# Reordering the first batch of a pooled-attention, gMLP and expert kernel, and the start of its second stage

## The chip, the cores and the metric

The kernel runs on one core of a Trainium2 chip. The metric is the device time of one execution in microseconds (us), as the median of several runs. The engines are PE (TensorE, matmul), DVE (VectorE), ACT (ScalarE), POOL (GpSimd) and SP (SyncE, which only issues DMAs here).

## The reference

Three blocks follow one another, in fp32, for 8 batches of 576 tokens:

```python
def _attn_ref(q, k, v):                       # 8 heads of 64
    k_p = k.reshape(B, H, S // 8, 8, D).mean(axis=3)      # 72 pooled keys
    v_p = v.reshape(B, H, S // 8, 8, D).mean(axis=3)
    scores = 1 / np.sqrt(D) * np.matmul(q, k_p.transpose(0, 1, 3, 2))
    ...                                       # softmax
    return np.matmul(attn, v_p)

def _moe_ref(x, w_in, g_ln, w_sg, b_sg, w_out):           # x: 576 x 512
    h = gelu(x @ w_in)                        # 1024 columns
    u, v = h[..., :512], h[..., 512:]
    v_n = (v - mu) / np.sqrt(var + 1e-06) * g_ln
    v_s = np.einsum('ts,bsd->btd', w_sg, v_n) + b_sg[None, :, None]
    return x + (u * v_s) @ w_out

def _moe2_ref(x, w_gate, wq, wk, wv, wo):     # 4 experts, each a causal attention head
    logits = x @ w_gate                       # the two best experts of each token
    ...                                       # softmax over the two
    for e in range(E):
        q, k, v = x @ wq[e], x @ wk[e], x @ wv[e]
        ye = causal_softmax(q @ k.T / 8) @ v @ wo[e]
        out += weight_of_e * ye
```

## The kernel before

Every fp32 operand is split into a high and a low half, and a product is three matmuls (high by high, high by low, low by high). Names that end in h or l (x2h and x2l, wih and wil, vnh and vnl) are such halves.

The program has two stages. `PhaseA` does attention and the gMLP block batch by batch and writes its result, x2h and x2l, to DRAM. `PhaseB` reads that back and does the experts. Within a batch of `PhaseA` the work on PE is: scores of the next batch's attention, v's half of the input product, u's half (`upart`, `up` tiles, columns 0 to 3 called U0 to U3), the normalisation of v (`norm`), the spatial products d0 to d3 (`spatial`, `sp` tiles), and the four columns of the output product (`outp`, `op` tiles), between which the probabilities of the next batch are transposed (`trans`, `tr` tiles, tiles 0 to 4). Then the next batch's attention output (`av`) is multiplied, and the loop goes on.

Batch 0 has nothing before it, so its order is written by hand in the string `SEQ`. In it W0 to W7 split the input weights (`load64`: some DVE and ACT operations, the last of which, line 130, writes the low half; W3 is the last of them in the string, and U3 needs it), S0 to S4 load and split the spatial weights (`load_ws`; low halves by `tensor_sub` at line 163, on POOL or DVE by the string `SE`), k pools the keys of batch 1 on POOL (`pool_k`, lines 176 to 180, 4 instructions for each of two halves), o0 to o3 load pieces of the output weights and O0 to O3 split them, N0, N2, N4 are the normalisation of token tiles 0 and 1, 2 and 3, and 4, C0 to C4 are the scores of batch 1, X and F its softmax, P0 to P3 the spatial products, and R and v load and pool batch 1's values (two halves vraw, then vlraw).

A scheduler decides the order on each engine from the order of the code and from waits for buffers. Two pools matter here. The tag "raw" has three buffers, which the raw keys, the raw values and the pieces of the output weights take in turn, so that a load waits until an older tenant was used: the first v load of batch 1 takes over from piece O1 of the output weights, each v load after it waits for the pooling of one before, and the loads of batch 2's keys and values wait for the pooling of batch 1's. The tag "x2" has four, for x2h and x2l of two columns: column 2 can be written only when column 0 has left for DRAM. All these DMAs are issued by SP, in its queue's order.

The normalisation of a tile pair goes from DVE (statistics mv) to POOL (lines 391 and 392, the inverse deviation rs) to ACT (line 400, vnh) to DVE (line 402, vnl; for tile 4 line 404), and spatial product d0 needs them tile by tile.

`PhaseB` begins with the items of the string `PRE` (v0 to v4 are value projections, g the gate, 00 to 03 and 10 to 13 the projections of q in two halves and k in two halves for head pairs 0 and 1), then goes through units of scores (line 839), softmax, scaling (line 860), transposes (line 886) and products, with items of `FIRSTF` for batch 0 between them (x0 to x3 load the next batch's x).

Of the kernel before, what the change touches and what calls it, by code (L numbers as in the profile page):

```python
# [12 lines left out]
AF = mybir.ActivationFunctionType  # L13
# [16 lines left out]
FD = {(0, 0), (0, 1), (1, 3), (1, 4)}  # L30
XA = (0, 1, 2, 3)
VE = ('PPP', 'PPP')
KE = ('DD', 'PP')
SE = 'PDPP'
SEQ = ("a0 a1 b0 d0 b3 b1 b2 d1 b4 d2 c g p0 h0 h1 p1 h2 h3 s0 e0 f0 s1 e1 f1 s2 s3 e2 f2 e3 f3 "
       "s4 e4 f4 y0 y1 y2 t0 t1 t2 t3 t4 z l W0 U0 W1 U1 W2 U2 K Q k o0 o1 W4 Y0 W5 Y1 W6 Y2 W7 Y3 S2 S1 S0 "
       "V4 W3 N0 U3 S4 N2 S5 N4 S3 C0 C1 o2 O0 P0 C2 X0 X1 F0 o3 O1 P1 C3 F1 X2 O2 R P2 F2 X3 O3 "
       "P3 C4 F3 X4 v")
# [3 lines left out]
class PhaseA:  # L42
# [69 lines left out]
    def load64(self, tv, hi, lo):  # L112
# [16 lines left out]
        nc.vector.scalar_tensor_tensor(lf, zh, 2.0 ** 32, zl, op0=OP.mult, op1=OP.add)  # L129
        nc.vector.scalar_tensor_tensor(lo, lf, 2.0 ** -52, gf, op0=OP.mult, op1=OP.mult)  # L130

# [149 lines left out]
    def av(self, b, steps):  # L281
# [8 lines left out]
        for x in steps:  # L290
# [15 lines left out]
            for p in range(NP):  # L306
                if p in done and "r" in done and (b, p) not in self.X32:
                    self.put_x(b, p, ps[p])

    def put_x(self, b, p, ps):  # L310
# [11 lines left out]
        nc.vector.tensor_sub(fh[:, S:], ps[:, 1, HS - 64:HS], fh[:, 512:S].bitcast(F32))  # L322
        if b == 0 and p in XA:
            nc.scalar.activation(x32, ps[:, :, :HS], AF.Copy)  # L324
        else:
            nc.gpsimd.tensor_add(x32, xh.bitcast(F32), xl.bitcast(F32))
# [80 lines left out]
    def upart(self, b, f):  # L407
# [3 lines left out]
        for h in range(2):  # L411
            s = slice(h * HS, h * HS + HS)
            o = ps[:, h, :HS]
            for kc in range(4):
                xh, xl = self.XH[b, kc][:, s], self.XL[b, kc][:, s]
                nc.tensor.matmul(o, self.wi[0][:, kc, c], xh, start=kc == 0, stop=False)  # L416
                nc.tensor.matmul(o, self.wi[0][:, kc, c], xl, start=False, stop=False)  # L417
                self.upmm = nc.tensor.matmul(o, self.wi[1][:, kc, c], xh, start=False, stop=kc == 3).ins  # L418
# [49 lines left out]
    def run(self):  # L468
        self.weight_tiles()
        for b in range(B):  # L470
# [4 lines left out]
            else:  # L475
                self.middle(b)
            if n + 1 < B:
                self.load_k(n + 1)
                self.load_v(n + 1, 0)
                self.load_q(n + 1)  # L480
            ahead = 1 if b else 0
            for f in range(4):
                if more:
                    if f == 0:
                        self.finish(n, 4)
                    self.trans(n, f + ahead)
                self.outp(b, f)
            if more:
                if not ahead:
                    self.trans(n, 4)  # L490
                self.av(n, (0, "r", 2, 1, 3))

    def first(self):

        done = {}
        def after(i):
            return self.tc.issue_after(done[i]) if i in done else nullcontext()
# [6 lines left out]
        def pool_k1():  # L504
            with after(4):
                self.pool_k(1)
        def load_v1():
# [108 lines left out]
FILL = (('', '12 10 11', '', '13 x0 x1 x2 x3', '', '', 'o3 o1 o0', '', ''), ('v0', 'v1 00 02', '01 o2', '03', '', '', '', 'v2 v3', 'v4 g'))  # L616
FIRSTF = (('10', '11', '12', '13 x0 x1 x2 x3', '', '', '', '', ''), ('v0 00', '', '01 02 v1', '03', '', '', '', 'v2 v3', 'v4 g'))
LASTF = (('', '10 12 11', '', '', '13', '', 'o1', '', 'o0'), ('', '', '', '', '', 'o2', '', '', 'o3'))
SDF = {(0, 0), (0, 1), (0, 5), (0, 8), (1, 0), (1, 2), (1, 7)}
SDL = {(0, 4), (0, 6), (1, 6), (1, 7)}  # L620
PRE = 'v0 00 01 02 03 v1 v2 v3 v4 g'
AVS = [(0, 256), (256, S)]
# [394 lines left out]
```

## Time and profile before

| | |
|---|---|
| median of 3 runs | 958.4 us (958.32 to 1010.67) |
| profiled execution, its own time | 959.46 us |
| its span | 957.7 us |
| PE, busy | 911.7 us, 95% of the span |
| DVE, busy | 694.4 us, 73% |
| ACT, busy | 517.8 us, 54% |
| POOL, busy | 444.9 us, 46% |

The profiled execution lies 1.06 us above the median, and 1.8 us of it are outside the span. A busy engine is one that executes; what the idle time of an engine is worth depends on whether anything that ends last waits for it. The granted clock is a share of TensorE's full 2.4 GHz; 0.5 is its lower level, 1.2 GHz.

### The profile page before, as it was taken

What the parts mean: (1) busy time and instruction counts of PE and PEld (TensorE: products, weight loads), DVE (VectorE), ACT (ScalarE), POOL (GpSimd) and SP (SyncE); (2) the same over time, 40 slices, a digit from 0 to 9 for tenths busy, and PEclk for the clock granted to TensorE, in tenths of its full rate; (3) what the DMA queues carried; (4) which work ended last, traced back from release to release, by engine and by line L of the source; (5) the groups of instructions that cost most, each with busy time, mean ns of one, the idle gap of its engine ahead of it and who ended that gap; (6) DMA issues with size and microseconds to landing.
All of it is one profiled execution on the core that took longest, in us unless ns stands there. A gap on an engine that the chain in (4) does not pass through costs nothing.

```text
span 957.7 us, 18439 instructions
## 1 busy us (share of the span) xinstructions
PE 911.7 (95%) x6488; PEld 864.2 (90%) x6488; DVE 694.4 (73%) x1876; ACT 517.8 (54%) x1285; POOL 444.9 (46%) x621
## 2 busy tenths in 40 slices
PE   4897789999999999999999999899999999999997
PEld 3677769989989999899899899899999999999987
DVE  6998838757667577587576614897879797878785
ACT  3765334344343443343443433777778776867776
POOL 6555747558469368375583560122222222323221
PEclk9798989999999999999999999999999999999999
DMA  9601522312402404223116014525353534435121
GB/s 326 241 13 44 178 98 74 132 61 72 155 28 73 170 12 143 100 72 133 62 51 196 22 40 135 144 48 165 88 163 91 160 101 128 137 91 165 49 62 75
DMA packets 51644, 102.86 MB, mean 107 GB/s; under 512 B 10592, under 2 KB 16736, under 8 KB 50656
## 3 DMA queue, kind: packets, MB, share of 16 engines
q1 hardware_dynamic: 51408, 101.68, 33.2%
q8 instruction: 52, 0.85, 0.4%
q14 instruction: 40, 0.33, 0.1%
q10 hardware_dynamic: 144, 0.00, 0.0%
HBM read 59.72 MB, written 28.31 MB: 92 GB/s over the span
## 4 chain that ended last, share of the span: by engine, by line
PE 76%; DVE 11%; ACT 4%; POOL 3%; DMA 3%; issue 2%; SPq 1%; ACTq 0%; POOLq 0%; DVEq 0%
PE av L906 4%; PE sc L224 3%; PE op L457 3%; PE sp L434 3%; PE sp L433 3%; PE sp L432 3%; PE up L416 3%; PE up L418 3%; PE up L417 3%; PE op L458 3%; PE op L459 3%; PE vp L355 3%; PE vp L356 3%; PE vp L357 3%; PE t L886 3%; PE pj L715 2%
## 5 line engine op out<-in xcount | busy, mean ns | idle before, releaser
L860 POOL TENSOR_SCALAR pr<-pr,sm,gw 128x128 f32<-128x128 f32 (+3 forms) x119 | 72.2, 608 | 210.4 <-DVE sm L856 135.7
L844 ACT ACTIVATE pr<-s,sm 128x256 f32<-128x256 f32 (+4 forms) x160 | 83.0, 520 | 41.3 <-DVE sm L841 19.5
L432 PE MATMUL sp<-wsh,vnh 128*128 128x288 f32 x256 | 78.7, 308 | 3.9 <-ACT vnh L400 3.9
L457 PE MATMUL op<-g,woh 128*128 128x288 f32 x256 | 77.4, 306 | 3.8 <-DVE x2l L464 3.1
L416 PE MATMUL up<-x,wih 128*128 128x288 f32 x256 | 76.9, 300 | 1.5 <-ACT xu L324 1.5
L433 PE MATMUL sp<-wsh,vnl 128*128 128x288 f32 x256 | 77.0, 301 | 0.7 <-DVE vnl L402 0.6
L458 PE MATMUL op<-g,woh 128*128 128x288 f32 x256 | 76.1, 298 | 1.4 <-DVE g L445 1.4
L434 PE MATMUL sp<-wsl,vnh 128*128 128x288 f32 x256 | 76.7, 300 | 0.0
L418 PE MATMUL up<-x,wil 128*128 128x288 f32 x256 | 75.9, 296 | 0.7 <-DVE wil L130 0.7
L713 PE MATMUL pj<-xbh,wqh 128*128 128x288 f32 x256 | 75.5, 295 | 0.0
L715 PE MATMUL pj<-xbh,wql 128*128 128x288 f32 x256 | 75.5, 295 | 0.0
L714 PE MATMUL pj<-xbl,wqh 128*128 128x288 f32 x256 | 75.4, 295 | 0.0
L417 PE MATMUL up<-x,wih 128*128 128x288 f32 x256 | 75.1, 293 | 0.0
L459 PE MATMUL op<-g,wol 128*128 128x288 f32 x256 | 74.7, 296 | 0.0
L841 DVE CUSTOM_DVE_ANT_0 s<-s,mk 128x512 f32<-128x512 f32 (+3 forms) x128 | 62.4, 488 | 3.3 <-PE t L886 3.0
L891 DVE TENSOR_TENSOR pbl<-t,pbh 128x512 fp32r<-128x512 f32 (+3 forms) x128 | 60.5, 484 | 2.5 <-ACT pbh L890 0.9
L224 PE MATMUL sc<-kbd,qt 128*128 128x144 f32 (+1 forms) x320 | 50.4, 304 | 11.7 <-DMA qt<-q_in 8.5
L886 PE MATMUL t<-ident,pr 128*128 128x128 f32 x320 | 56.3, 277 | 3.3 <-POOL pr L860 3.1
L906 PE MATMUL av<-pbh,vt 128*128 128x320 f32 (+4 forms) x224 | 55.9, 279 | 2.7 <-ACT pbh L890 2.7
L464 POOL TENSOR_TENSOR x2l<-x2l,x2h 128x576 fp32r<-128x576 f32 x8 | 11.4, 1430 | 99.3 <-ACT x2h L463 99.3
L224 PEld LDWEIGHTS sc<-kbd,qt 128*128 128x128 f32 (+1 forms) x320 | 44.5, 192 | 14.4 <-issue 10.8
L400 ACT ACTIVATE vnh<-vg,rs 128x512 fp32r<-128x512 f32 (+1 forms) x40 | 27.2, 718 | 53.1 <-POOL rs L392 40.5
(247 smaller groups left out, 3352.4 us busy)
## 6 DMA issues: line engine op xcount, KB each, us to landing
kraw<-k_in SPq DMA_DIRECT2D x16, 576.0 KB, 3.8
x<-x2h SPq DMA_DIRECT2D x32, 288.0 KB, 2.1
x<-x2l SPq DMA_DIRECT2D x32, 288.0 KB, 2.1
xbl<-x SPq DMA_DIRECT2D x32, 288.0 KB, 4.1
xbh<-x SPq DMA_DIRECT2D x32, 288.0 KB, 4.0
kd<-scr SPq DMA_DIRECT2D x64, 144.0 KB, 2.5
out<-o SPq DMA_DIRECT2D x32, 288.0 KB, 3.8
vraw<-v_in SPq DMA_DIRECT2D x16, 512.0 KB, 4.1
```

Source lines behind the costliest of these rows:

```text
L224: nc.tensor.matmul(ps[:m, p // 2, (p % 2) * 144:(p % 2) * 144 + 144], qt[:, p, o:o + m], kbd[:, p, :], start=p % 2 == 0, stop=True, skip_g ...
L416: nc.tensor.matmul(o, self.wi[0][:, kc, c], xh, start=kc == 0, stop=False)
L417: nc.tensor.matmul(o, self.wi[0][:, kc, c], xl, start=False, stop=False)
L418: self.upmm = nc.tensor.matmul(o, self.wi[1][:, kc, c], xh, start=False, stop=kc == 3).ins
L432: nc.tensor.matmul(o, vh[:, k, c], self.ws[0][:, k, s], start=k == 0, stop=False)
L433: nc.tensor.matmul(o, vl[:, k, c], self.ws[0][:, k, s], start=False, stop=False)
L434: nc.tensor.matmul(o, vh[:, k, c], self.ws[1][:, k, s], start=False, stop=False)
L457: nc.tensor.matmul(o, self.wo[0][:, k, c], gh[:, s], start=k == 0, stop=False)
L458: nc.tensor.matmul(o, self.wo[0][:, k, c], gl[:, s], start=False, stop=False)
L459: nc.tensor.matmul(o, self.wo[1][:, k, c], gh[:, s], start=False, stop=k == 3)
L715: nc.tensor.matmul(ps, self.wq[1][:, kc, c], xh[:, s], start=False, stop=kc == 3)
L906: nc.tensor.matmul(ps[:, s - lo:], vt[:, j, 2 * p + e].rearrange("p a d -> p (a d)"), t[:, e, j * PTS + s:j * PTS + up], start=j == 0 and ...
```

## The change

In batch 0, the pooling of batch 1's keys (k) goes behind W3 in `SEQ` and waits there for W3's last DVE operation, by way of two small copies on DVE into the raw keys; load o1 goes with it. The low halves of the spatial weights are all computed on DVE (`SE`). The copies of x that the residual uses (x32, line 324) are written after all of `av`. The loads of batch 2's keys, values and queries are written behind the columns of the output product, not ahead of them. For every batch `upart` takes its four row blocks in the order 2, 0, 1, 3. The second stage begins with all value projections and the gate, then the keys, then the queries and pair 1's queries, and its first units lose three fillers.

```diff
-SE = 'PDPP'
+SE = 'DDDD'
...
-       "s4 e4 f4 y0 y1 y2 t0 t1 t2 t3 t4 z l W0 U0 W1 U1 W2 U2 K Q k o0 o1 W4 Y0 W5 Y1 W6 Y2 W7 Y3 S2 S1 S0 "
-       "V4 W3 N0 U3 S4 N2 S5 N4 S3 C0 C1 o2 O0 P0 C2 X0 X1 F0 o3 O1 P1 C3 F1 X2 O2 R P2 F2 X3 O3 "
+       "s4 e4 f4 y0 y1 y2 t0 t1 t2 t3 t4 z l W0 U0 W1 U1 W2 U2 K Q o0 W4 Y0 W5 Y1 W6 Y2 W7 Y3 S2 S1 S0 "
+       "V4 W3 k o1 N0 U3 S4 N2 S5 N4 S3 C0 C1 o2 O0 P0 C2 X0 X1 F0 o3 O1 P1 C3 F1 X2 O2 R P2 F2 X3 O3 "
...
-        nc.vector.scalar_tensor_tensor(lo, lf, 2.0 ** -52, gf, op0=OP.mult, op1=OP.mult)
+        self.cv = nc.vector.scalar_tensor_tensor(lo, lf, 2.0 ** -52, gf, op0=OP.mult, op1=OP.mult).ins
...
+        for p in range(NP if b == 0 else 0):
+            self.nc.scalar.activation(self.X32[b, p], ps[p][:, :, :HS], AF.Copy)
...
-        if b == 0 and p in XA:
-            nc.scalar.activation(x32, ps[:, :, :HS], AF.Copy)
-        else:
+        if b:
             nc.gpsimd.tensor_add(x32, xh.bitcast(F32), xl.bitcast(F32))
...
-            for kc in range(4):
+            for kc in (2, 0, 1, 3):
...
-            if n + 1 < B:
-                self.load_k(n + 1)
-                self.load_v(n + 1, 0)
-                self.load_q(n + 1)
+            def loads():
+                if n + 1 < B:
+                    self.load_k(n + 1)
+                    self.load_v(n + 1, 0)
+                    self.load_q(n + 1)
+            if b:
+                loads()
...
                 self.outp(b, f)
+            if not b:
+                loads()
...
         def pool_k1():
-            with after(4):
-                self.pool_k(1)
+            with self.tc.issue_after(self.cv):
+                for t in self.RAW["k", 1].values():
+                    self.nc.vector.tensor_copy(t[:, 0, 0, :2], t[:, 0, 0, :2])
+            self.pool_k(1)
...
-FIRSTF = (('10', '11', '12', '13 x0 x1 x2 x3', '', '', '', '', ''), ('v0 00', '', '01 02 v1', '03', '', '', '', 'v2 v3', 'v4 g'))
+FIRSTF = (('', '12', '', '13 x0 x1 x2 x3', '', '', '', '', ''), ('v0 00', '', '01 02 v1', '03', '', '', '', 'v2 v3', 'v4 g'))
...
-PRE = 'v0 00 01 02 03 v1 v2 v3 v4 g'
+PRE = 'v0 v1 v2 v3 v4 g 02 03 00 01 10 11'
```

What this does to the order on the engines is seen at three places. On POOL, in batch 0, around the pooling of batch 1's keys (kraw into kbd), the low halves of the spatial weights (wsl) and the first normalisation (rs); the list of before begins with the second half of the keys, ahead of which the same rows stand once more for the first half:

```order
L176 TENSOR_TENSOR kraw<-kraw 128x576
L177 TENSOR_TENSOR kraw<-kraw 128x288
L180 TENSOR_TENSOR kbd_96<-kraw 64x2x72 x2
L163 TENSOR_TENSOR wsl<-st_594,wsh 128x576
L163 TENSOR_TENSOR wsl<-st_602,wsh 128x576
L163 TENSOR_TENSOR wsl<-st_704,wsh 128x576
L391 TENSOR_SCALAR rs<-mv 128x2
L392 TENSOR_TENSOR rs<-rs,mhalf 128x2
```

After:

```order
L175 TENSOR_TENSOR kraw<-kraw 128x576 x2
L176 TENSOR_TENSOR kraw<-kraw 128x288 x2
L179 TENSOR_TENSOR kbd_96<-kraw 64x2x72 x4
L390 TENSOR_SCALAR rs<-mv 128x2
L391 TENSOR_TENSOR rs<-rs,mhalf 128x2
```

The three weight operations have left POOL, and the pooled keys (both halves, eight instructions) stand directly ahead of the first rs, which was behind the weights.

On SP, in batch 0, after the last piece of the output weights, before (vraw and vlraw are batch 1's values in the first two rows; kraw, the vraw rows behind it and qt are batch 2's; x_0_57 is the DRAM buffer of batch 0's x2):

```order
L71 DMA vraw<-v_in 128x1024 x2
L75 DMA vlraw<-vl_in 128x512
L58 DMA kraw<-k_in 128x1152 x2
L71 DMA vraw<-v_in 128x1024
L65 DMA qt<-q_in 128x2304
L71 DMA vraw<-v_in 128x1024
L466 DMA x_0_57<-x2h 128x576
L466 DMA x_0_57<-x2l 128x576
```

After:

```order
L70 DMA vraw<-v_in 128x1024 x2
L74 DMA vlraw<-vl_in 128x512
L64 DMA qt<-q_in 128x2304
L57 DMA kraw<-k_in 128x1152 x2
L70 DMA vraw<-v_in 128x1024
L465 DMA x_0_57<-x2h 128x576
L465 DMA x_0_57<-x2l 128x576
L70 DMA vraw<-v_in 128x1024
```

The queries went ahead of batch 2's keys, and the first x2h and x2l ahead of the last value load; the other loads still stand ahead of the write-back.

On SP at the start of the second stage, before (kd is a copy of the projected keys of a head pair, four DMAs; qz pieces of the queries; xbh and xbl the loads of batch 1's x):

```order
L737 DMA qzvhi_6015<-qs_6007 64x512
L737 DMA qzvlo_6016<-qs_6007 64x512
L751 DMA kd<-scr 64x576 x4
L737 DMA qzvn_6017<-qs_6011 64x512
L737 DMA qzgln<-qs_6011 64x512
L642 DMA xbh<-x_1_58 128x576
L751 DMA kd<-scr 64x576 x4
L643 DMA xbl<-x_1_58 128x576 x2
L644 DMA xbh<-x_1_58 128x64
```

After:

```order
L757 DMA kd<-scr 64x576 x4
L743 DMA qzvhi_6017<-qs_6009 64x512
L743 DMA qzvlo_6018<-qs_6009 64x512
L743 DMA qzvn_6019<-qs_6013 64x512
L743 DMA qzgln<-qs_6013 64x512
L648 DMA xbh<-x_1_58 128x576
L650 DMA xbh<-x_1_58 128x64
L649 DMA xbl<-x_1_58 128x576 x2
L757 DMA kd<-scr 64x576 x4
```

The first kd moved ahead of the queries' pieces, and the second behind two more of the loads of x.

## Rows read from the trace of the kernel before

**Rows 1.** Busy time, granted clock and transfers in five stretches (engine: us, instructions).

```profile
76.00:83.20 7.20, 6.54 (x25) 5.96 (x26) 6.41 (x13) 5.59 (x20) 0.11 (x1) 0.54 0.01 1
83.20:120.20 37.00, 30.66 (x224) 28.95 (x223) 32.18 (x58) 15.53 (x50) 27.06 (x36) 1.00 0.45 149
120.20:123.90 3.70, 0.05 (x1) 0.00 (x0) 1.12 (x3) 0.65 (x1) 0.00 (x0) 1.00 0.74 288
123.90:131.00 7.10, 7.06 (x34) 5.42 (x35) 2.06 (x5) 1.66 (x3) 1.53 (x2) 0.53 0.39 149
...
300.00:500.00 200.00, 200.00 (x1414) 188.84 (x1414) 136.81 (x233) 79.94 (x115) 130.11 (x180) 1.00 0.26 89
```

**Rows 2.** What PE waited for from 30 to 150 us: us, times, longest.

```profile
PE sp L432 <- ACT vnh L400: 3.9, 2, 3.4
PE tr L275 <- DVE ptl L278: 3.7, 1, 3.7
PE op L457 <- DVE x2l L464: 2.8, 1, 2.8
PE up L416 <- ACT xu L324: 1.5, 1, 1.5
```

**Rows 3.** PE in order of time: start us, us, work, idle before it and releaser.

```profile
79.93 0.61 PE L435 MATMUL sp<-wsh,vnh 128*128 128x288 f32 x1 [0.41 <-DVE vnh L404]
...
132.58 0.40 PE L355 MATMUL vp<-wih,x 128*128 128x512 f32 x1
```

**Rows 4.** POOL in order of time, same columns.

```profile
30.42 1.88 POOL L176 TENSOR_TENSOR kraw<-kraw 128x576 f32<-128x576 f32 x1
...
37.76 1.09 POOL L180 TENSOR_TENSOR kbd<-kraw 64x144 f32<-64x144 f32 x2
52.37 11.77 POOL L163 TENSOR_TENSOR wsl<-st,wsh 128x576 fp32r<-128x576 f32 x3 [13.51 <-ACT xu L420]
67.07 0.63 POOL L391 TENSOR_SCALAR rs<-mv 128x2 f32<-128x2 f32 x1 [2.93 <-DVE mv L390]
...
102.15 1.27 POOL L191 TENSOR_TENSOR vraw<-vraw 128x512 f32<-128x512 f32 x1
...
106.49 0.99 POOL L198 TENSOR_TENSOR vlo<-vraw,vhi 64x128 fp32r<-64x128 f32 x2
...
111.28 1.40 POOL L176 TENSOR_TENSOR kraw<-kraw 128x576 f32<-128x576 f32 x1 [0.20 <-DMA kraw<-k_in]
...
113.63 1.04 POOL L180 TENSOR_TENSOR kbd<-kraw 64x144 f32<-64x144 f32 x2
```

**Rows 5.** DVE in order of time, same columns.

```profile
52.73 0.75 DVE L163 TENSOR_TENSOR wsl<-st,wsh 128x576 fp32r<-128x576 f32 x1
...
64.35 0.68 DVE L130 SCALAR_TENSOR_TENSOR wil<-st,g 128x512 fp32r<-128x512 f32 x1
...
79.12 0.75 DVE L404 SCALAR_TENSOR_TENSOR vnh<-vg,rs,vnh 64x512 fp32r<-64x512 f32 x1
...
85.26 0.69 DVE L130 SCALAR_TENSOR_TENSOR wol<-st,g 128x512 fp32r<-128x512 f32 x1
...
154.46 3.65 DVE L404 SCALAR_TENSOR_TENSOR vnh<-vg,rs,vnh 64x512 fp32r<-64x512 f32 x1 [1.53 <-ACT vnh L400]
```

**Rows 6.** ACT in order of time, same columns.

```profile
122.08 0.65 ACT L463 ACTIVATE x2h<-op 128x576 fp32r<-128x576 f32 x1 [4.26 <-DMA x<-x2h]
```

**Rows 7.** SP's DMA issues in order of time: start, us of the issue, transfer.

```profile
115.08 0.42 SPq L466 DMA_DIRECT2D x<-x2h  x1
```

**Rows 8.** The page's DMA issues over the whole span: median us from issue to landing.

```profile
kraw<-k_in SPq DMA_DIRECT2D x16, 576.0 KB, 3.8
x<-x2h SPq DMA_DIRECT2D x32, 288.0 KB, 2.1
...
vraw<-v_in SPq DMA_DIRECT2D x16, 512.0 KB, 4.1
```

**Rows 9.** What PE waited for from 575 to 700 us.

```profile
PE t L886 <- POOL pr L860: 2.4, 3, 1.0
```

More of the change, by code (lines that the diff above doesn't have):

```diff
@@ L30 @@
 FD = {(0, 0), (0, 1), (1, 3), (1, 4)}
-XA = (0, 1, 2, 3)
 VE = ('PPP', 'PPP')
 KE = ('DD', 'PP')
-SE = 'PDPP'
+SE = 'DDDD'
 SEQ = ("a0 a1 b0 d0 b3 b1 b2 d1 b4 d2 c g p0 h0 h1 p1 h2 h3 s0 e0 f0 s1 e1 f1 s2 s3 e2 f2 e3 f3 "
-       "s4 e4 f4 y0 y1 y2 t0 t1 t2 t3 t4 z l W0 U0 W1 U1 W2 U2 K Q k o0 o1 W4 Y0 W5 Y1 W6 Y2 W7 Y3 S2 S1 S0 "
-       "V4 W3 N0 U3 S4 N2 S5 N4 S3 C0 C1 o2 O0 P0 C2 X0 X1 F0 o3 O1 P1 C3 F1 X2 O2 R P2 F2 X3 O3 "
+       "s4 e4 f4 y0 y1 y2 t0 t1 t2 t3 t4 z l W0 U0 W1 U1 W2 U2 K Q o0 W4 Y0 W5 Y1 W6 Y2 W7 Y3 S2 S1 S0 "
+       "V4 W3 k o1 N0 U3 S4 N2 S5 N4 S3 C0 C1 o2 O0 P0 C2 X0 X1 F0 o3 O1 P1 C3 F1 X2 O2 R P2 F2 X3 O3 "
        "P3 C4 F3 X4 v")
@@ L413, in upart @@
             o = ps[:, h, :HS]
-            for kc in range(4):
+            for kc in (2, 0, 1, 3):
                 xh, xl = self.XH[b, kc][:, s], self.XL[b, kc][:, s]
-                nc.tensor.matmul(o, self.wi[0][:, kc, c], xh, start=kc == 0, stop=False)
+                nc.tensor.matmul(o, self.wi[0][:, kc, c], xh, start=kc == 2, stop=False)
                 nc.tensor.matmul(o, self.wi[0][:, kc, c], xl, start=False, stop=False)
```

## The prediction

> **What bounds the kernel now.** I read the table of stretches first, for what PE does. In the steady batches it has no gap: from 300 to 500 us it is busy for 200.00 of 200 us at a granted clock of 1.00 [rows 1]. Nothing that the change does to DVE, POOL or the transfers there can shorten the run unless it takes PE work away, and it takes none. So I went to the places where PE waits, which are batch 0 and the start of the second stage. PE's waits up to 150 us name four [rows 2]: 3.9 us in the normalisation (ACT's vnh), 3.7 us once for a low half of the transposed probabilities (ptl), 2.8 us for x2l in the output columns, 1.5 us for a copy of x ahead of U0. Then the clock: from 76 to 83.2 us it is 0.54 and from 123.9 to 131 us 0.53, each time just after a long wait of PE, while the stretch between, with the wait of 2.8 us in it, stays at 1.00 [rows 1]. A stretch of 7.06 busy us at 0.53 costs 7.06 x 0.47 = 3.3 us. The second long wait together with its clock is thus worth 3.7 + 3.3 = 7.0 us, the largest single thing that the change could take.
>
> What ends that second wait is a transfer. ACT had nothing to do for 4.26 us until x2h of column 0 had reached DRAM [rows 6], since column 2 takes its buffer; DVE's x2l and the ptl behind it in DVE's queue came after that, and PE's transposes after those. The DMA had been issued at 115.08 us [rows 7], so that it took almost 7 us, where the median over the run is 2.1 [rows 8]: the loads of batch 2 were ahead of it, 1.2 MB of queries among them. And it was issued that late because SP stood at a value load that waits for pooled keys, which POOL finished at 113.63 + 1.04 = 114.67 us [rows 4].
>
> **The copies of x and the order of the row blocks: 0.** On ACT the copies stand in the same sequence before and after, and U0 waits in both for the same one, since it frees U0's PSUM tile. The bound below is the whole 1.5 us; above it is small, because the block that is asked for first is ready first.
>
> **Spatial weights on DVE: 0 on the path.** DVE gets three more of 0.75 us [rows 5], 2.25 us; POOL loses one stretch of 11.77 us [rows 4]. The low half of W3 ended at 64.35 + 0.68 = 65.03 us [rows 5], after a stretch in which DVE shared time with those POOL operations. How much DVE gets back there has no row; the same line 404 takes 0.75 us alone and 3.65 us beside POOL's value pooling [rows 5], so between nothing and more than the 2.25 us. I take W3's end at 64 us (bounds 63 and 67.3). Either way U3 ends before PE must wait for the normalisation, so the gain is covered by that wait.
>
> **Pooled keys behind W3: +1.5 on the first spatial product.** They were done in the shadow of batch 0's attention, 30.42 to 38.85 us, 8.4 us for eight instructions; a single half alone in a later batch took 111.28 to 114.67, which makes 6.8 for two [rows 4]. Now they start on POOL at about 64.2 and end between 71.0 and 72.6. Behind them in POOL's queue is the first rs, which began at 67.07 [rows 4], and behind that the chain vnh, vnl, the aggregation for the next pair, rs, vnh, vnl, and the same for tile 4, whose low half was ready at 79.12 + 0.75 = 79.87 us and which PE took at 79.93 [rows 3, 5]. The scores of batch 1 wait for the keys as well. Not all of the 3.9 to 5.5 us arrives: about 2 us of statistics stood between and are now ahead of the first vnl on DVE. I count 9 us from the end of the first rs (72.4 to 74.3) to the last low half, 81.4 to 83.3 us, so +1.5 to +3.4, and I take the lower end because DVE is less disturbed than before (bounds 0 and +5.5). PE is idle meanwhile, which costs the clock as before; that is no new loss.
>
> **Output weights, value pooling and write-back: -2.8 for the first batch.** Since the pieces of w_out come later, their splitting moves behind d0 and d1 on DVE. The last operation of O1 was over at 85.95 us [rows 5]; in the new order it stands behind d1's product, two reductions of scores and its own four operations, which brings it to 94.8. The first value load waits for exactly that. From there: a v load of 4.1 us [rows 8] to 98.9; pooling, 102.15 to 107.48 before, so 5.3 us [rows 4], to 104.2; the second v load to 108.3; pooling to 113.6; batch 2's keys, 3.8 us [rows 8], to 117.4; their first half pooled, 3.4 us, at 120.8. Before it was 114.67, so this chain on POOL and SP slides by 6 us. Only the first pair of x2 profits from standing ahead of the last value load: it waits for vlraw's pooling instead, some 115.5 us, and is issued at about 116, hardly another moment than 115.08. But the queries have been loaded by then, so I give it 4 us in place of 7, and the transposes of tile 4 begin near 122 and not at 123.9, some half us after the columns (120.2 + 1.5). The second pair is issued at 121.3 and needs between 2.1 (the median) and 4.1 us (a v load is just ahead); with 3.1 it lands at 124.4. The last column's sum on DVE needs its buffer, and the ptl of tile 4 stands behind that sum: 1.5 us, 125.9. Now the rest of av. Before, from the end of the wait to the first matmul of batch 1's v at 132.58 [rows 3] there were 8.7 us, 5.4 without the clock's 3.3, 0.5 of them transposes; 32 of av's 40 matmuls now stand behind the last ptl, so 0.8 x 4.9 = 3.9 us, if the clock stays up. That gives 129.8 in place of 132.58: -2.8. I take the clock as staying up, since two short waits of 0.5 and some 2 us take the place of one of 3.7, and after the one of 2.8 us in the columns it was 1.00 [rows 1, 2]. The bounds are -7.0 (wait and clock wholly gone) and +3 (this chain later by another 3 us and the clock low as before).
>
> **Second stage: -1.2.** PE has the same matmuls. Its waits there for scaled scores of POOL sum to 2.4 us in three pieces, the longest 1.0 [rows 9]. With the gate's small operations out of DVE's way earlier, the first units should be scaled sooner; but the second pair's kd now stands behind more loads on SP. Bounds -2.4 (all of it) and +1.0 (one more wait like the longest); I take half the gain.
>
> **Sum.** 0 + 0 - 2.8 - 1.2 = -4.0 us (the +1.5 is inside the chain). The profiled execution took 959.46 us, which gives 955.5; the median lies 1.06 lower, so I forecast **954.4 us**, with 952 to 956.5 for this case, chance 0.40.
>
> **The rivals.** *The POOL chain keeps pace.* If O1 is split earlier than I count, the loads and both x2 pairs are on time, the whole 7.0 us goes: 958.4 - 7.0 - 1.2 = 950.2. For it speaks that DVE is less disturbed, against it that four splits now crowd behind d0. Chance 0.18. *The second stage gives nothing or loses up to 1.0*, because the kd copies come later: 955.6 to 956.6; chance 0.16. *The change does not do what it says*: the order shows that most loads are still ahead of the write-back, so the wait of 3.7 us and the low clock may simply stay; then only -1.2, 957.2. Chance 0.10.
>
> *Slower: the pooled keys are held up on POOL.* They now run beside DVE's statistics and normalisation, with the first rs right behind them. The row against them is the three weight operations, 3.92 us each [rows 4] beside a busy DVE, where the first step of pooled keys, of the same 128x576, took 1.40 [rows 4], 2.8 times less. Each us by which they end later moves d0, O1, the value loads and the end of av by one. From +2.8 the first batch gains nothing, and if PE's wait there is then as long as the two after which the clock was low, its 3.3 us are lost too: with +4, -2.8 + 4 + 3.3 - 1.2 = +3.3, 961.7 us; chance 0.12. With the whole factor of 2.8 they take 19 in place of 6.8 us, +12.2, which makes -2.8 + 12.2 + 3.3 - 1.2 = +11.5, 969.9; chance 0.04. Against it stands that in batch 0's attention the same keys needed only 8.4 us beside a DVE at work.
>
> [...]
>
> **How the numbers follow.** 949 to 960.5 us should hold the time 8 times in 10: it takes in the forecast, the first three rivals and the mild half of a late chain, and leaves out most of the slow rival and a second stage at its lower bound on top of the whole 7.0. Two per cent is 19 us here, about what a measurement of this kernel can tell from no change; no case reaches it but something unforeseen, so 0.02 for faster, 0.96 for within, 0.02 for slower.
>
> **What would show it right or wrong.** In the profile after: pooled keys on POOL near 64 to 72 us and the first rs directly behind; d0 about 1.5 us later; the first x2h issued near 116 and the second near 121; no wait of PE over 3 us between 118 and 126 and a clock near 1.00 behind it; batch 1's v at about 129.8; the second stage's waits for line 860's successor about halved. The prediction is wrong if the normalisation ends much beyond 83 us, if the second pair of x2 comes past 123, or if the clock is low behind the columns once more.

## The result: slower by about one per cent

The changed kernel took 971.85 us (median of 3 runs, 969.26 to 973.09) where the kernel before took 958.4. The ratio, on record as of fast runs without the slow one of 1010.67 us, is 1.0112 with an interval of [1.0087, 1.0137]; that of the two medians would be 1.014. The forecast was 954.4 us, in a range up to 960.5: the time lies outside it, on the other side of no change.

The profiled execution, the slowest of the three, took 973.09 us with a span of 971.3, 13.6 more than that of before. It splits in two at points that both traces have. Batch 1's first matmul of v begins at 141.04 us, 8.46 later than in [rows 3]. The second stage begins at 591.92 us and not at 583.40, which is the same 8.5, so nothing is lost or won in the batches between. The second stage itself then lasts 379.4 us in place of 374.3, 5.1 more, in this execution.

Line numbers after the change are mostly lower by one up to the loads, and higher by six in the second stage. First PE, of its waits from 40 to 160 us those that answer to [rows 2] or are new (us, times, longest), and its first matmul of batch 1's v:

```profile
PE sc L223 <- POOL kbd L179: 2.8, 1, 2.8
PE av L295 <- DVE x2l L461: 2.7, 1, 2.7
PE op L456 <- DVE x2l L463: 2.4, 1, 2.4
PE sp L434 <- DVE vnh L403: 2.4, 1, 2.4
...
PE tr L274 <- DVE ptl L277: 1.6, 1, 1.6
```

```profile
141.04 0.40 PE L354 MATMUL vp<-wih,x 128*128 128x512 f32 x1
```

The wait of 3.7 us for ptl is down to 1.6, as hoped. But 2.8 us for the pooled keys are new, and the wait of `av` for x2l (2.7) stands where that of ptl stood. No wait is over 3 us any more, and yet everything is late. So I looked where the time of the first spatial product went, on POOL (start us, us, work, idle before and releaser):

```profile
65.31 2.82 POOL L175 TENSOR_TENSOR kraw<-kraw 128x576 f32<-128x576 f32 x2 [33.41 <-DVE kraw L511]
...
70.49 2.14 POOL L179 TENSOR_TENSOR kbd<-kraw 64x144 f32<-64x144 f32 x4
72.72 0.23 POOL L390 TENSOR_SCALAR rs<-mv 128x2 f32<-128x2 f32 x1
...
127.15 1.03 POOL L179 TENSOR_TENSOR kbd<-kraw 64x144 f32<-64x144 f32 x2
```

The pooled keys take 65.31 to 72.63 us, eight instructions in 7.3 us, and the first rs, at 67.07 in [rows 4], follows at 72.72. On DVE the last low half of the normalisation ends at 83.28 + 0.74 = 84.02 us (79.87 in [rows 5]), and piece O1 of the output weights ends at 98.91 (85.95):

```profile
83.28 0.74 DVE L403 SCALAR_TENSOR_TENSOR vnh<-vg,rs,vnh 64x512 fp32r<-64x512 f32 x1
...
98.24 0.67 DVE L129 SCALAR_TENSOR_TENSOR wol<-st,g 128x512 fp32r<-128x512 f32 x1
...
133.70 0.76 DVE L461 TENSOR_TENSOR x2l<-op,xu 128x576 f32<-128x576 f32 x1 [3.72 <-DMA x<-x2h]
```

The last of these rows shows what is left of the write-back: the last column's sum waits 3.72 us for a transfer of x2. Its DMA was issued at 128.59 us, the first of the pair's two, so about 5 us before. On DVE the pair's low half, and on SP the DMAs:

```profile
120.81 0.76 DVE L463 TENSOR_TENSOR x2l<-op,x2h 128x576 fp32r<-128x576 f32 x1 [0.78 <-ACT x2h L462]
```

```profile
121.22 0.42 SPq L465 DMA_DIRECT2D x<-x2h  x1
...
128.21 0.33 SPq L70 DMA_DIRECT2D vraw<-v_in  x1
128.59 0.43 SPq L465 DMA_DIRECT2D x<-x2h  x1
```

In [rows 7] the first x2h was issued at 115.08; now it is 121.22. The second pair was ready at 120.81 + 0.76 = 121.57, and stood for 7 us in SP's queue behind the value load that waits for the pooled keys (127.15 + 1.03 = 128.18). Last, the stretches that answer to [rows 1] (busy us and instructions of PE, PEld, DVE, ACT and POOL, granted clock, DMA share, GB/s):

```profile
71.50:84.00 12.50, 8.17 (x32) 6.38 (x32) 8.20 (x16) 5.08 (x8) 4.59 (x9) 0.73 0.25 84
...
119.30:126.40 7.10, 7.10 (x44) 7.08 (x45) 3.48 (x7) 2.06 (x3) 3.64 (x8) 0.76 0.80 248
126.40:130.10 3.70, 2.12 (x17) 1.89 (x16) 1.42 (x3) 0.65 (x1) 1.65 (x3) 1.00 0.64 185
130.10:134.50 4.40, 1.73 (x10) 1.18 (x10) 0.80 (x2) 0.45 (x2) 0.00 (x0) 0.86 0.93 342
134.50:141.00 6.50, 6.49 (x35) 5.66 (x36) 2.26 (x6) 2.53 (x4) 3.13 (x3) 0.57 0.26 101
```

From 76 to 83.2 us the clock was 0.54 before [rows 1], and from 71.5 to 84 it is 0.73 now. Later it is low twice: 0.76 with PE busy for all of 119.3 to 126.4 us, and 0.57 while the last matmuls of `av` run. The low clock that the change was to save is still there, and a second, milder one has come ahead of it.

### The profile page after: what moved, and what is told of

Same layout as the page of the kernel before. It is cut to its first block, busy times and chain, and to the rows that moved or that the text cites. A ratio compares the mean times of both kernels' runs of the same rounds, so it can differ in the third digit from the quotient of the medians.

```text
span 971.3 us, 18445 instructions
## 1 busy us (share of the span) xinstructions
PE 916.7 (94%) x6488; PEld 869.7 (90%) x6488; DVE 691.0 (71%) x1881; ACT 518.1 (53%) x1285; POOL 431.8 (44%) x618
## 4 chain that ended last, share of the span: by engine, by line
PE 75%; DVE 10%; ACT 4%; DMA 4%; issue 3%; POOL 2%; SPq 1%; ACTq 0%; DVEq 0%; POOLq 0%
PE sc L223 4%; PE av L912 4%; PE op L456 3%; PE sp L432 3%; PE sp L433 3%; PE sp L431 3%; PE up L415 3%; PE up L417 3%; PE up L416 3%; PE op L457 3%; PE op L458 3%; PE vp L354 3%; PE vp L355 3%; PE vp L356 3%; PE t L892 2%
## 5 line engine op out<-in xcount | busy, mean ns | idle before, releaser
L275 ACT ACTIVATE pth<-tr 128x640 fp32r<-128x640 f32 (+1 forms) x40 | 26.2, 654 | 57.6 <-PE tr L274 48.0
```

## The experiments

The theory after this result was that the pooled keys cost the time, since they were taken out of the shadow of batch 0's attention and now stand ahead of the first rs. The rivals were the weights (with what they do to the order on SP), the strings of the second stage, and the copies and loads. Each expectation names its theories in its own words. The kernel before, run beside these, had medians of 959.95 to 960.84 us, and all but one of its single runs lay between 955 and 965; so a time read from one profile is worth less than a ratio over several runs.

**The weights alone** (`weights_alone`):

```diff
-SE = 'PDPP'
+SE = 'DDDD'
```

> The kernel before with only the string SE changed: all low halves of the spatial weights on DVE; the pooled keys stay where they were. Theory A (the first batch loses its 8.5 us because the pooled keys stand ahead of the first rs): the value loads and the write-back change places as in the changed kernel, but the normalisation ends at about 80 us as before, and the time is within 2 us of before, 956 to 960. Theory B (the loss comes from the pieces of the output weights being split later on DVE, so that the first value load of batch 1 and all that POOL does after it slide): most of the 8.5 us is here already, 964 to 967, with O1's last operation at 95 us or later.

It took 962.15 us, ratio 1.0031 [1.0011, 1.0051]. The order shows that this one string also makes the later changes on SP: queries ahead of keys, and the first x2 pair ahead of the last value load. DVE and SP in order of time:

```profile
81.03 0.76 DVE L438 TENSOR_TENSOR xu<-sp,xu 128x576 f32<-128x576 f32 x1 [0.96 <-PE sp L436]
...
92.08 0.68 DVE L130 SCALAR_TENSOR_TENSOR wol<-st,g 128x512 fp32r<-128x512 f32 x1
```

```profile
121.11 0.43 SPq L466 DMA_DIRECT2D x<-x2h  x1
```

d0's product with u (line 438, the first work behind d0) starts at 81.03 us; before it was 83.87:

```profile
83.87 0.76 DVE L438 TENSOR_TENSOR xu<-sp,xu 128x576 f32<-128x576 f32 x1 [1.40 <-PE sp L436]
```

So the weights help the normalisation, by 2.8 us in this pair of profiles. Over all profiles the gain is smaller and less sure: d0's product starts at 80.84 and 84.06 in the two other kernels below with only the weights' side of the front changed, and at 82.92 to 85.01 in four with the front as before. But O1 ends 6.8 us later than in [rows 5] all the same, because its operations now stand behind d0 and, most of them, behind d1 on DVE; the second x2 pair is issued at 121.11 (116.02 before), the clock is 0.73 from 126.3 to 132.7 us, and batch 1's v begins at 132.71, as before. What the front gains, the chain of output weights, values and write-back takes back, and the time lies between the ranges of the two theories.

**Weights and keys** (`weights_and_keys`: the last edit, and the keys as in the change):

```diff
-       ... U2 K Q k o0 o1 W4 Y0 ...
-       "V4 W3 N0 U3 ...
+       ... U2 K Q o0 W4 Y0 ...
+       "V4 W3 k o1 N0 U3 ...
...
-            with after(4):
-                self.pool_k(1)
+            with self.tc.issue_after(self.cv):
+                for t in self.RAW["k", 1].values():
+                    self.nc.vector.tensor_copy(t[:, 0, 0, :2], t[:, 0, 0, :2])
+            self.pool_k(1)
```

> The kernel before with the weights on DVE and the pooled keys behind W3, nothing else. Theory A: this holds the whole loss of the first batch, 8 to 9 us above before (966.5 to 967.5), and 8 above the run with the weights alone. Theory B: at most 2 to 3 us above the run with the weights alone.

969.5 us, 1.0103 [1.0079, 1.0127]. PE's scores of batch 1 and the first spatial matmuls, and d0's product on DVE:

```profile
70.92 2.44 PE L224 MATMUL sc<-kbd,qt 128*128 128x144 f32 x8 [2.80 <-POOL kbd L180]
73.91 1.28 PE L432 MATMUL sp<-wsh,vnh 128*128 128x288 f32 x2 [0.55 <-ACT vnh L400]
```

```profile
86.66 0.76 DVE L438 TENSOR_TENSOR xu<-sp,xu 128x576 f32<-128x576 f32 x1 [1.75 <-PE sp L436]
```

The keys, with the load o1 that goes with them, put d0 from 81.03 to 86.66, 5.6 us later, and what hangs on d0 by as much: O1 ends 5.6 us later, at 98.38, the first x2h is issued 5.4 later, at 120.69, and batch 1's v begins at 139.43 and not at 132.71. In all six profiles with the keys in this place, those below among them, d0's product starts between 86.66 and 87.48. The medians of the two runs differ by 7.35 us, near the 8 of Theory A. The ratio is nearly that of the whole change, and v's delay most of its 8.46 us in the first batch.

**The second stage alone** (`stage2_alone`) and **x alone** (`x_alone`: the copies behind `av` and the order 2, 0, 1, 3); the first two pairs of lines are of the one, the rest of the other:

```diff
-FIRSTF = (('10', '11', '12', ...
+FIRSTF = (('', '12', '', ...
-PRE = 'v0 00 01 02 03 v1 v2 v3 v4 g'
+PRE = 'v0 v1 v2 v3 v4 g 02 03 00 01 10 11'
...
+        for p in range(NP if b == 0 else 0):
+            self.nc.scalar.activation(self.X32[b, p], ps[p][:, :, :HS], AF.Copy)
...
-            for kc in range(4):
+            for kc in (2, 0, 1, 3):
```

> The kernel before with only the second stage's two strings changed. Theory A (the fillers taken out from between the first nine units and the later kd of pair 1 leave PE waiting and lower its clock): +5 us, 963 to 964, with a wait of some 2.7 us for kd. Theory B (the second stage loses only because the first ends later, for instance by transfers that then collide): within 1 us of before, 957.5 to 959.5.

> The kernel before with only the copies of x written after av and the new order of row blocks in the u products. Both theories: no engine's order of instructions moves, only the operands of the u products, so 957.5 to 959.5; a gain of up to 1.5 us would show that the wait ahead of U0 ends with its first row block and not with the PSUM tile.

960.34 us, 1.0000 [0.998, 1.0019], and 960.49 us, 1.0002 [0.9979, 1.0025]. In the profile of `stage2_alone` the second stage lasts 373.85 us. Neither part costs or gives anything by itself that these runs can tell, which is some 2 us either way. The part on the loads needed no run: with the loads written behind the columns and nothing else changed, the order on every engine stays that of before, word for word.

**Keys behind the normalisation's rs** (`keys_after_rs`). If the only harm is that rs stands behind the keys on POOL, this mends it:

```diff
-       "V4 W3 N0 U3 S4 N2 S5 N4 S3 C0 C1 o2 O0 P0 ...
+       "V4 W3 N0 U3 S4 N2 S5 N4 S3 k o1 C0 C1 o2 O0 P0 ...
...
-            with after(4):
+            with self.tc.issue_after(self.rs):
```

with the new `SE`, and `k` and `o1` gone from their old places.

> The weights on DVE as in weights_alone, and the pooled keys of batch 1 moved behind the last rs of batch 0 on POOL (near 80 us), so that they can't hold up the normalisation. Theory A (what the pooled keys cost is the first rs behind them): d0's product at 81 to 82 us as in weights_alone, and its time, 960 to 963. Theory B (what they cost is what waits for the keys themselves: the first scores of batch 1 and, by the shared raw buffers, the load and splitting of O1 and the value loads behind it): d0 at 81 to 82 us, but O1's last operation at 98 us or later, as with the keys behind W3, and 967 to 971.

971.76 us, 1.0116 [1.0085, 1.0147]: no better. The first rs begins at 66.98, as before the change, but now PE stops:

```profile
83.94 1.33 PE L224 MATMUL sc<-kbd,qt 128*128 128x144 f32 x4 [5.82 <-POOL kbd L180]
```

The scores C0 stand ahead of d0 in PE's queue and wait 5.8 us for the keys; d0's product starts at 89.61, where both theories had 81 to 82. So the rs was not the sole gate. Nor were the scores the only new one. On DVE, beside the pooling (POOL from 78.12 us), the last low half was late as well:

```profile
77.75 4.90 DVE L127 TENSOR_SCALAR g<-a 128x512 uint32<-128x512 uint32 x1
82.68 0.86 DVE L404 SCALAR_TENSOR_TENSOR vnh<-vg,rs,vnh 64x512 fp32r<-64x512 f32 x1
```

It was ready at 83.54 us, 0.4 before the scores could start, and in `weights_alone` at 78.54.

**The scores behind d0 in the code** (`keys_scores_late`: as the last, with C0 and C1 written behind P0):

```diff
-       ... S3 k o1 C0 C1 o2 O0 P0 C2 ...
+       ... S3 k o1 o2 O0 P0 C0 C1 C2 ...
```

> As keys_after_rs, the pooled keys behind the last rs and the weights on DVE, and also the first two scores of batch 1 (C0, C1) behind the first spatial product in the code. Theory A (the pooled keys cost their time because C0 and C1 stand in PE's queue ahead of the spatial products): d0's product back at 81 to 83 us, no wait of PE for keys above 2 us, and 3 to 7 us below keys_after_rs (971.8), 965 to 969. Theory B (they cost it through the later softmax, values and write-back, whatever PE does in between): d0 early, but within 2 us of keys_after_rs.

974.61 us, 1.0156 [1.0123, 1.019]. The scheduler put the scores ahead of d0 on PE all the same (they wait 5.7 us), so this run decides nothing on its question. The operation at line 127 took 4.91 us in it, at the same place.

**The scores really behind d1** (`keys_scores_behind`: keys behind the last rs, scores issued only after the last matmul of d1; in the string, shown against that of the last run, O1 and P1 move ahead of C0):

```diff
-       ... S3 k o1 o2 O0 P0 C0 C1 C2 X0 X1 F0 o3 O1 P1 C3 ...
+       ... S3 k o1 o2 O0 P0 o3 O1 P1 C0 C1 C2 X0 X1 F0 C3 ...
...
+            self.spmm = nc.tensor.matmul(o, self.vn2[:, c], self.ws[1][:, 4, s], start=False, stop=True).ins
...
+        def score1(i):
+            with self.tc.issue_after(self.spmm):
+                self.score(1, i)
```

> Weights on DVE, pooled keys behind the last rs, and now the scores C0 to C4 of batch 1 really behind spatial products on PE (the first behind d0 and d1), so that neither the rs nor PE's queue has the keys ahead of it. Theory A (the pooled keys cost by standing in these two queues ahead of d0): d0's product at 81 to 83 us, and no wait of PE for keys over 1 us; the first batch then ends where the later softmax lets it, within 3 us of keys_after_rs or below. Theory B (the time is lost elsewhere, for instance by POOL's pooling slowing the normalisation's DVE operations): d0 at 86 us or later here as well.

964.69 us, 1.0049 [1.0032, 1.0066]. Better by 6 to 7 us than `keys_after_rs`, and some 2 us by the ratios above `weights_alone`. PE waits for no keys now. It waits 5.4 us for the last low half of the normalisation, and DVE shows why, with POOL beside it:

```profile
77.02 0.68 DVE L125 SCALAR_TENSOR_TENSOR a<-st,g 128x512 uint32<-128x512 uint32 x1
77.73 4.91 DVE L127 TENSOR_SCALAR g<-a 128x512 uint32<-128x512 uint32 x1
82.67 0.86 DVE L404 SCALAR_TENSOR_TENSOR vnh<-vg,rs,vnh 64x512 fp32r<-64x512 f32 x1
```

```profile
78.10 2.75 POOL L176 TENSOR_TENSOR kraw<-kraw 128x576 f32<-128x576 f32 x2
80.82 1.54 POOL L177 TENSOR_TENSOR kraw<-kraw 128x288 f32<-128x288 f32 x2
```

An operation at line 127 that takes 0.42 us in the median of its 12 took 4.91, from 77.73 to 82.64 us, while POOL pooled keys from 78.10. The last low half stands behind it, and d0's product comes at 87.83, as late as Theory B had it. With the queues of POOL and PE out of the way, DVE is the third gate. It is there in all three runs with the keys behind the last rs (4.90, 4.91 and 4.91 us). What the scores cost in PE's queue is the rest: PE's work on the last low half starts at 83.58 here and at 86.42 in `keys_after_rs`, 2.8 us.

**The write-back's transfers.** Is the wait of 3.7 us in [rows 2] made by SP's queue, which issues x2 late, or by the transfers that are in flight? `store_act` is the kernel before with batch 0's x2 issued from ACT, so that no load stands ahead of them in a queue:

```diff
-            nc.sync.dma_start(self.x2d[b][:, f, i], ...
+            (nc.scalar if b == 0 else nc.sync).dma_start(self.x2d[b][:, f, i], ...
```

> The kernel before, with only batch 0's x2h and x2l written to DRAM by DMAs issued from ACT's queue instead of SP's, right behind the operation that makes them. Theory A (the wait of 3.7 us and the low clock behind it come from the write-back standing in SP's queue behind loads that wait for POOL): the first x2h leaves near 111 us and not 115, the wait at the last transposes falls under 1.5 us, the clock stays near 1.00, and the time falls by 5 to 7 us. Theory B (they come from the transfers of batch 2's loads, which the write-back shares the DMA engines with wherever it is issued): the first x2h lands at 119 us or later, and the time is within 2 us of before.

959.88 us, 1.0001 [0.9985, 1.0016]. ACT, and the stretches behind it (columns as above):

```profile
112.12 0.35 ACTq L466 DMA_DIRECT2D x<-x2h  x1
...
121.74 0.65 ACT L463 ACTIVATE x2h<-op 128x576 fp32r<-128x576 f32 x1 [2.61 <-DMA x<-x2h]
```

```profile
115.00:120.00 5.00, 5.00 (x41) 5.00 (x40) 3.07 (x5) 1.65 (x3) 0.96 (x2) 1.00 1.00 366
120.00:125.00 5.00, 1.56 (x12) 1.33 (x10) 1.12 (x3) 0.65 (x1) 0.00 (x0) 1.00 0.86 343
125.00:130.00 5.00, 4.96 (x27) 3.36 (x27) 1.19 (x3) 1.01 (x2) 1.40 (x1) 0.59 0.47 180
```

The first x2h left 3 us earlier, at 112.12, and column 2's x2h began at 121.74, as good as the 122.08 of [rows 6], though the front of this execution ran 1.1 us later (d0's product at 85.01). From 115 to 120 us the DMA engines are busy for 1.00 of the time, and the clock is 0.59 behind it. Against that, `q_held` leaves the queue as it is and takes 1.2 MB out of the flight: the queries of batch 2 are loaded only when the last column's x2h is written, by a small copy of it into their tile.

```diff
-                self.load_q(n + 1)
+                if b:
+                    self.load_q(n + 1)
...
+                if b == 0 and f == 3:
+                    self.QT[n + 1] = self.w.tile([128, NP, S], F32, name="qt")
+                    self.nc.vector.tensor_copy(self.QT[n + 1][:, 0, :2], self.hi[:, 0, :2])
+                    self.load_q(n + 1)
```

> The kernel before, with the load of batch 2's queries (1.2 MB) made to wait for x2h of batch 0's last column, by a small copy on DVE into its tile: what the move of the loads behind the columns says, for the one load that can be moved. Theory A (the wait of 3.7 us at the last transposes is the transfer of x2 among batch 2's loads): the first x2h, issued at 115 us as before, lands in 3 to 4 us and not in 7, the wait falls to 1 us or less and the clock behind it stays near 1.00: 5 to 7 us below before, 953 to 955. Theory B (it is the late issue, behind the value load that waits for POOL): within 2 us of before.

957.06 us, 0.9972 [0.9953, 0.999]. SP, ACT and PE in order of time:

```profile
115.00 0.59 SPq L467 DMA_DIRECT2D x<-x2h  x1
...
125.37 0.37 SPq L65 DMA_DIRECT2D qt<-q_in  x1
```

```profile
119.98 0.65 ACT L463 ACTIVATE x2h<-op 128x576 fp32r<-128x576 f32 x1 [0.70 <-DMA x<-x2h]
```

```profile
121.85 0.49 PE L275 MATMUL tr<-ident,P 64*128 64x64 f32 x5
...
127.63 0.39 PE L355 MATMUL vp<-wih,x 128*128 128x512 f32 x1
```

With x2h issued at the same 115.00 us as before, the buffer is free after 5.0 us and not 7.0, column 2 waits 0.70 us and not 4.26, tile 4's transposes begin at 121.85 without a wait, the clock is 1.00 from 120 to 130, and batch 1's v begins 4.95 us earlier than in [rows 3]. The run gains some 3 us, less than the 5 to 7 of Theory A and more than Theory B allows.

Not all of these 4.95 us can be put down to the transfers. `x_alone` leaves the order on every engine as it was, so its profile is nearly another execution of the kernel before. In it x2h is issued at 114.11 and column 2's x2h begins at 121.16, again after 7 us. Yet the transposes wait only 0.95 us, and v begins 3.75 us earlier than in [rows 3]. Here the clock was low ahead of the wait and not behind it (columns as above):

```profile
110.00:115.00 5.00, 3.39 (x15) 3.40 (x16) 3.64 (x7) 1.35 (x2) 3.30 (x5) 0.58 0.93 322
115.00:120.00 5.00, 5.00 (x31) 5.00 (x31) 1.56 (x4) 0.70 (x1) 0.00 (x0) 0.73 0.98 351
120.00:125.00 5.00, 4.05 (x29) 3.31 (x27) 2.66 (x6) 1.67 (x3) 0.31 (x1) 1.00 0.63 242
```

```profile
123.02 0.49 PE L275 MATMUL tr<-ident,P 64*128 64x64 f32 x5 [0.95 <-DVE ptl L278]
...
128.83 0.39 PE L355 MATMUL vp<-wih,x 128*128 128x512 f32 x1
```

In the profile of `q_held` the clock is 0.77 from 115 to 120 us as well. So the length of this wait and the place of the low clock change from one execution to the next, and what the transfers are worth is read from the medians: 3 us. In the kernel before they were the cause, and an earlier issue alone gave nothing.

**Combinations.** `weights_store_act` is the weights with x2 on ACT; `weights_q_held_act` adds `q_held` to it; `after_store_act` is the changed kernel with x2 on ACT. The edits are the lines shown above for `weights_alone`, `store_act` and `q_held`.

> The weights on DVE as in weights_alone, and the write-back of batch 0 issued from ACT's queue. Theory A: the 2.8 us that the normalisation won in weights_alone reach the end of the first batch: another 2 to 3 us below store_act, 7 to 10 below before. Theory B: as weights_alone, 0 to 3 us above before.

> Weights on DVE, queries held back as in q_held, write-back of batch 0 from ACT's queue. In weights_store_act no wait of PE names a transfer any more, so Theory A gives no further gain: 956 to 958. Theory B the same; a gain of more than 2 us over weights_store_act (957.0) would show that the loads still cost the columns something.

> The changed kernel with the write-back of batch 0 issued from ACT's queue. Theory A: what the sliding value loads did to the write-back is gone, what the pooled keys did to the normalisation (3 to 4 us) stays: 1 to 4 us above before, some 7 below the changed kernel. Theory B: within 2 us of the changed kernel, 10 to 13 above before.

957.03 us, 0.9966 [0.995, 0.9981]; 957.72 us, 0.998 [0.9964, 0.9997]; 963.77 us, 1.0036 [1.0018, 1.0053]. With the weights, whose order has the queries earlier, x2 from ACT does help: no engine waits for a transfer of x2 any more, the clock is 1.00 from 125 to 131 us, and batch 1's v begins at 131.11. The two remedies don't add up. In the changed kernel x2 on ACT takes away most of the loss, some 7 us by the ratios, and v begins at 134.19; but d0 stays late, at 87.09. So in these kernels, where the second pair stands behind the value load that waits for pooled keys, the late issue does cost, unlike in the kernel before.

**The second stage once more.** `after_stage2_back` is the changed kernel with the old `PRE` and `FIRSTF` (the lines of `stage2_alone`, taken back). `after_act_again` and `after_act_stage2_back` are the same pair with x2 on ACT, in more runs.

> The changed kernel with the second stage's two strings as before. Theory A (the second stage's strings cost nothing, as in stage2_alone, and the 5 us in the profiled execution were a slow transfer of kd in that execution): within 1.5 us of the changed kernel, 970 to 973, with the second stage itself at 374 to 376 us. Theory B (with the later first stage they do cost): 3 to 5 us below the changed kernel, 966 to 969.

> after_store_act once more, for comparison with the next run on the same chip. Both theories: 961 to 965, with the second stage at 376 to 379 us if the strings of the second stage cost time in this setting, at 374 to 375 if not.

> after_store_act with the second stage's strings as before. Theory A (the strings cost nothing, and a slow kd is chance): within 1 us of after_act_again. Theory B (with the strings of the change the second kd, issued behind more loads, is needed just when it lands, and costs 1 to 4 us in many executions): 1.5 to 4 us below it.

967.56 us, 1.0092 [1.0062, 1.0122] (1.0112 with the new strings); 962.97 us, 1.0030 [1.0013, 1.0046]; 961.49 us, 1.0015 [1.0001, 1.0029]. Both pairs come out nearer Theory B, with 4.3 and 1.5 us between the medians. The first pair has three and four runs, not taken side by side, and 1.9 us by the ratios; in the second, twelve runs against twelve side by side, the means differ by 1.1 us (0.3 to 2.0 when the runs are resampled). In the profiles the second stage lasts 374.3, 374.9 and 375.3 us with the old strings (the kernel before and the two runs here), and 379.4, 377.9 and 374.4 with the new ones (the changed kernel, `after_store_act` and `after_act_again`). So behind the changed first stage the strings cost something in some executions, about 1 us in the mean with x2 on ACT; how much in the changed kernel itself is not settled. The waits of PE at the start of the second stage in the changed kernel (560 to 700 us; us, times, longest), and one of `after_store_act`:

```profile
PE s L833 <- DMA kd<-scr: 2.7, 1, 2.7
PE t L879 <- DVE sm L861: 1.5, 1, 1.5
PE t L892 <- POOL pr L866: 1.5, 1, 1.5
```

```profile
PE s L833 <- DMA kd<-scr: 1.2, 1, 1.2
```

The wait for scaled scores, 2.4 us in three pieces in [rows 9], is 1.5 in one, so what I hoped for there did come in part. But one wait of 2.7 us for a pair's kd, issued from 614.69, and one of 1.5 for DVE are new; those four DMAs took 7.0 to 7.5 us, where the same pair's took 2.3 to 4.4 in the profile before. From 620 to 630 us PE was busy for 7.40 us at a clock of 0.66, before for 9.94 at 1.00. With the same strings they took 5.4 to 5.9 us in `after_store_act`, where PE waits 1.2 us for them, and 4.3 to 4.5 in `after_act_again`, where it doesn't wait.

## Why the prediction was wrong, point by point

- **Copies of x and row order, 0: right.** `x_alone` is at 1.0002 [0.9979, 1.0025].
- **Spatial weights, 0 on the path: too pessimistic on the spot.** W3 ended at 65.15 us, inside the bounds, later than the 64 taken. What they give is on the path behind it: d0's product 2.8 us earlier in `weights_alone`, with the spread named there. I had looked for the gain in U3 only, and folded the rest into "DVE is less disturbed".
- **Pooled keys, +1.5: this is the step that failed first.** On POOL they went as counted, 7.3 us to 72.63, at the upper end of 71.0 to 72.6, and were not stretched; the first rs ended at 73.04 + 0.71 = 73.75, inside 72.4 to 74.3. But from there to the last low half it took 10.3 us and not the 9 that I counted, so that it ended at 84.02, +4.15 and outside 81.4 to 83.3, though inside the outer bound of +5.5. I took the lower end of my own range, and gave the keys the weights' gain as well; alone they cost d0 5.6 us, and each step behind d0 as much. They lay for nothing in the shadow of attention, and beside the normalisation they hold it up in one of three ways: rs behind them on POOL (`weights_and_keys`), scores waiting for them on PE (`keys_after_rs`, where DVE was held too), or DVE held beside them (`keys_scores_behind`).
- **Output weights, values and write-back, -2.8: wrong by 11.3 us (+8.46).** The chain was the right one, and its steps are in the trace; each was late. O1 ended at 98.9 and not 94.8, the first half of batch 2's keys was pooled at 128.18 and not 120.8 (127.15 + 1.03), the first x2h went at 121.22 and the second at 128.59, where I had 116 and 121.3, and the second pair took about 5 us and not 3.1. The first pair, which I gave 4 us since the queries were in, took 7 (column 2's x2h waited until 128.28), with batch 2's keys and a value load issued at 119.23 and 120.84. `after_store_act` shows that the write-back's place in SP's queue costs some 7 us here, and `weights_store_act` against `weights_alone` some 6 without the keys; I had taken it for hardly any. With x2 on ACT the keys still cost some 5, by 1.0015 in `after_act_stage2_back` against 0.9966 in `weights_store_act`. Moreover I let the clock stay up, since no wait was as long as before; it was 0.76 and 0.57. In the kernel before, I had named both the late issue and the loads in flight behind the long wait; there `store_act` shows no gain from an earlier issue, and `q_held` some 3 us from fewer loads in flight, not the 7.0 that I put on the wait and its clock. That sum was read from one execution: in `x_alone` the wait is 0.95.
- **Second stage, -1.2: not shown, and of the wrong sign with the other parts.** Alone it is 0 within 2 us. Behind the changed first stage the strings cost about 1 us in the mean of the runs with x2 on ACT. The second pair's kd behind more loads, which I had named, is seen in two of three profiles as a wait of 2.7 and 1.2 us; I had bounded it at +1.0.
- **Loads behind the columns.** I had the right reading of the order there, that most loads still stand ahead of the write-back. The part does nothing by itself.

The time is that of the slower rival with a chance of 0.16 in all, 961.7 to 969.9 us and beyond, by another mechanism than its own: it had the keys stretched to 19 us by DVE, and they took 7.3. What was stretched was an operation of DVE, in the three runs with the keys behind the last rs, 4.91 in place of 0.42 us. The Trainium skill, page "SBUF — State Buffer", section "Who interferes with whom", has the second engine fully blocked, for one whole instruction of the other, when a DVE operation in a 2-port mode meets GpSimd at their shared ports. By the same section a tensor_scalar, as line 127 is, can enter such a mode when its operands meet certain conditions; that this one did no run shows. Here the delay lasted over four pooling instructions of POOL, more than the one that the page's lock covers. That these ports are the cause of the 4.91 us no run here shows; that it happens beside the pooling is in the rows.

What is shown: the keys' new place costs 7 us, by `weights_and_keys` against `weights_alone`, through d0 and all that follows it. The write-back's place in SP's queue costs another 6 to 7 us wherever the weights are on DVE, which is more than the weights give. And in the kernel before the write-back waits for transfers, by `q_held` against `store_act`. What stays open is what the second stage's strings cost in the changed kernel, what part of each loss is the clock's, and whether the keys have any free place between W3 and d1: no kernel here removed the three gates at once. Of all kernels tried `weights_store_act` and `q_held` are the best, both some 0.3% below the kernel before.

## What to carry to other kernels

The pooled keys were free in the shadow of a long stretch of another engine. Moved beside a chain of small steps over three engines they came onto that chain, whichever queue they were moved past. So look for every consumer ahead of the chain's end, in each queue, before taking a low price. When a store lands late, separate a late issue from a full flight before changing queues: issue it elsewhere once, and hold back the loads once, in the kernel at hand, since the answer was another one before and after the change. Read a wait from more than one execution before it becomes the largest term of a sum: the one of 3.7 us here was 0.95 in another. And read from the order what a change in the text does at all: one string of four letters moved more instructions here than the part that was written as a move.

## What was not expected of the hardware

A DVE operation of 128x512 with one input took 4.91 us and not 0.42 beside four POOL operations of 1.40, 1.40, 0.79 and 0.79 us, in each of three runs. A transfer of 288 KB of x2h, 2.1 us in the median, took about 7 us with batch 2's loads in flight, 1.2 MB of queries among them, and issuing it 3 us earlier from another engine brought it home at about the same time; the Trainium skill, page "DMA: Bandwidth & Descriptors", section "Issuing engines are not separate DMA queues", says that all transfers run on the same 16 DMA engines whoever starts them, and the busy share of 1.00 from 115 to 120 us agrees. And after waits of PE of 2.8 us and less, the clock still came out at 0.76 and 0.57 in the stretches behind, where the kernel before had 1.00 in a stretch with one of 2.8 in it [rows 1, 2].
